# RWKV attention, then balanced experts: a fourth expert's first layer by seven products, a GpSimd drain behind the last gather, the last block's results in two halves

## The chip, the cores and the metric
The kernel runs on one core of a Trainium2 chip. Its time is device microseconds for one execution, the median of several runs. TensorE does the matrix products, VectorE (DVE) and ScalarE (ACT) work on tiles, GpSimd (POOL) issues the indirect DMAs, SyncE (SP) issues the plain ones.

## The reference
Two parts follow each other. An RWKV-5 attention over 4 sequences of 768 steps gives 3072 rows of 384 numbers. A mixture of 8 experts then gives each row to one expert, exactly 384 rows each, and sends it through that expert's two layers:

```python
for idx in order:                      # all (token, expert) pairs by falling logit
    tok, e = int(idx) // E, int(idx) % E
    if assigned[tok] >= 0 or counts[e] >= cap:
        continue
    assigned[tok] = e
    counts[e] += 1
...
for e in range(E):
    mask = assigned == e
    h = np.maximum(x[mask] @ w1[e], 0.0)      # 384 x 384 by 384 x 1024
    out[mask] = h @ w2[e]                     # 384 x 1024 by 1024 x 384
```

All numbers are 32-bit floats.

## The kernel before
**Stages.** The first 115 us or so are the attention. Then come the experts, one after the other, in `Experts.run`. Which expert is full next, and with which rows, is found by a search on VectorE with small products on TensorE (`likely_steps`, lines 1026 to 1099): three rounds that count candidates, each with two products (L949, L960) between VectorE operations, then `acc` (L1072), which settles the expert's rows and is kept as `walk.taking`. Then `tokens` lists the row numbers, and `fetch` (L1535) gathers the rows by three indirect DMAs from GpSimd (`gather`, L1530) and loads the weights from SyncE (L1523).

**Numbers.** An expert with all its three blocks of 128 rows is called whole. The whole ones have n = 1 to 7; the fourth is n = 4. Two blocks of one expert are done during the attention ("early"), and its last block comes at the end as n = 8.

**What runs during what.** While `run` works on n, the search for n + 1 or for the one behind it is made. `later` is a generator whose steps are pulled by `next` at set points of n's work. For n = 3, nine steps are pulled; with the last of them the search that settles expert 5's candidate rows is over. At the start of n = 4 `ahead = next(...)` pulls the whole next search and `fetch(5)`.

**First layer.** Plainly (`hidden`, L1648) it is 8 x 3 products of 128 x 128 weights by 384 columns. By seven (`hidden_by_seven`, L1600) two of the three slabs of rows are multiplied as 2 x 2 blocks in seven products, the third slab is added in plain products: 11 block products, each in four parts of 192 columns. It needs four sums of weight blocks (`weight_sums`, L1572, 128 x 512 each), five sums of row blocks (`row_sums`, L1583, 128 x 192 each), six additions of results on VectorE (L1624) and copies and activations on ScalarE (L1616, L1620). Each 32-bit product shows as two MATMUL instructions in the trace. `FIRST_BY_SEVEN` (L1799) lists the experts that are done so: 2, 3, 6, 7. The weight sums of the next expert are put behind `summed`, an early sum of the second layer now under way; its row sums behind `walk.taking`.

**Second layer.** Two of the three blocks go by seven products (`seven`, L1711, with the S sums of hidden blocks and T sums of weight blocks, L1704), the third block plainly in `result` (L1787, sixteen instructions of 384 columns). For n = 6 and 7 all three blocks go by fifteen products (L1763).

**The next rows turned.** The rows of n + 1 are turned by DMA, except for n + 1 = 1 and 5 (`BY_TENSOR`), which TensorE turns (L1545) into PSUM and ScalarE copies. During n = 4 that turning stands in the second layer ahead of product P4 in the program.

**Order.** A planner at build time puts the instructions of each engine in order by expected times; at run time each engine keeps that order. `tc.issue_after(ins)` puts the instructions of its block behind `ins` in their engine's order, without a wait.

**The end.** After n = 8's `result` with `to is None` the results stand in `o_last`; a branch (L2023) decides whether the general path has to run, and then `x.scatter(o_last, tok_last, ...)` (L2040) writes the last 128 rows. The closing DRAINs and barrier carry line 2064.

Of the kernel before, what the change touches and what calls it, by code (L numbers as in the profile page):

```python
# [10 lines left out]
F32 = mybir.dt.float32  # L11
# [1452 lines left out]
def rwkv5_eagle_then_base_layer_balanced(  # L1464
# [12 lines left out]
    nc = tc.nc  # L1477
    N, DX = out.shape
    E, _, F = moe_w1.shape
# [4 lines left out]
    KF = F // 128  # L1484
# [7 lines left out]
    walk = Assignment(ctx, tc, LG, CAP, C)  # L1492
    out_rows = dram_disjoint_views(out, NT)
    o_last = keep.tile([128, DX], F32, name="o_last")
    tok_last = keep.tile([128, 1], I32, name="tok_last")
# [3 lines left out]
    class Experts:  # L1499
# [26 lines left out]
        def gather(self, n, tok, within=N):  # L1526
            nb = tok.shape[1]
            xg = self.turns[n % 2].tile([128, NC, DX], F32, name="xg")
            for c in range(nb):
                nc.gpsimd.indirect_dma_start(  # L1530
                    out=xg[:, c, :], out_offset=None, in_=x_dram[0:within, :],
                    in_offset=bass.IndirectOffsetOnAxis(ap=tok[:, c:c + 1], axis=0))
            return xg
# [251 lines left out]
                                         in_=o_sb, in_offset=None)  # L1785

        def result(self, c, hid, w2, tok, to):  # L1787
            o_ps = self.ps_o.tile([128, DX], F32, name="o_ps")
            for j in range(KF):
                nc.tensor.matmul(o_ps, hid[:, j, ts(c, 128)], w2[:, j, :], start=(j == 0), stop=(j == KF - 1))  # L1790
            if to is None:
                nc.scalar.copy(o_last, o_ps)
                nc.vector.tensor_copy(tok_last, tok[:, c:c + 1])
                return
            o_sb = self.o.tile([128, DX], F32, name="o_sb")
            nc.scalar.copy(o_sb, o_ps)
            self.scatter(o_sb, tok[:, c:c + 1], to)

        FIRST_BY_SEVEN = 2, 3, 6, 7  # L1799
        BY_TENSOR = 1, 5  # L1800

        def run(self, ahead, later, rows, pulls={}, xT=None):
            xT, lead = xT or self.turn(ahead), True
            row_sums = weight_sums = None
            while ahead:
                n, _, tok, w1, w2 = ahead
                nb = tok.shape[1]
                whole = nb == NC
                many = whole and n in (E - 2, E - 1)
                ahead = next((a for a in later if a), None)  # L1810
                if weight_sums and not row_sums:
                    with tc.issue_after(walk.taking.ins):
                        row_sums = self.row_sums(xT)
                sums = dict(row_sums, **weight_sums) if weight_sums else None
                row_sums = weight_sums = None
                after = ahead and ahead[0] in self.FIRST_BY_SEVEN and ahead[2].shape[1] == NC
                late, lead = lead and not many, False
# [31 lines left out]
                def progress(t):  # L1849
                    nonlocal weight_sums  # L1850
                    if after and t > 1.1 and not weight_sums:
                        with tc.issue_after(summed.ins):
                            weight_sums = self.weight_sums(ahead[3])
                    while due and t > due[0]:
                        due.pop(0)
                        next(later, None)
                        if many and not due:
                            turn()
# [4 lines left out]
                if sums:  # L1863
                    hid = self.hidden_by_seven(sums, sums, progress)
                    half(hid)
                else:
                    hid = self.hidden(w1, xT, nb * 128, half if whole else lambda hid: None, progress, late)
# [48 lines left out]
    with ExitStack() as whole:  # L1916
        x = Experts()
# [5 lines left out]
        with ExitStack() as part:  # L1923
# [20 lines left out]
            with tc.manual_schedule():  # L1944
# [13 lines left out]
                for m in (1, 5, 2, 5, 2, 6, 5):  # L1958
# [4 lines left out]
                tok = walk.tokens(first["place"])  # L1963
                walk.between = lambda: None
                xg = x.gather(1, tok)
                to = walk.in_order(tok)
# [7 lines left out]
                                                                tag=("kT_ps", "rT_ps")[c % 2]))  # L1974
# [10 lines left out]
        def later():  # L1985
            yield from search
            walk.bound(ident)
            now = second
            for n in range(2, 5):
                walk.book(now, first=True)  # L1990
                yield x.fetch(n, now["fmax"], walk.tokens(now["place"]))
                walk.leave(now)
                yield
                now = walk.new_outs()
                yield from walk.likely_steps(**now)
            was = now
            walk.book(was)
            walk.leave(was)
            for n in range(5, E):
                rest = n == E - 1  # L2000
                yield
                if rest:
                    yield
                    now = walk.remainder()
                else:
                    now = walk.new_outs()
                    yield from walk.likely_steps(**now)
                walk.book(now, surely=rest)
                walk.choose(was, now)
                yield x.fetch(n, was["fmax"], walk.tokens(was["place"]))  # L2010
                if not rest:
                    walk.leave(now)
                was = now
            yield
            yield
            tc.mark_branch_hint_location("whole")
            have["ok"] = walk.found()
            yield x.fetch(E, walk.star, walk.tokens(walk.star_place, 1))

        x.run(ahead, later(), (a for a in [*out_rows[2:NT - 1], None]),  # L2020
              {1: 5, 2: 7, 3: 9}, xT)

    with tc.If(have["ok"] < 1, label="whole", preferred_fallthrough_block=False):  # L2023
# [3 lines left out]
        with ExitStack() as arm:  # L2027
            x = Experts()
# [40 lines left out]
```

## Time and profile before

| | us |
|---|---|
| median of 3 runs | 388.47 (388.26 to 389.25) |
| the profiled execution | 387.69 |
| its span, first to last instruction | 386.0 |
| TensorE busy | 369.8 |
| VectorE busy | 273.2 |
| ScalarE busy | 190.6 |
| GpSimd busy | 142.7 |

The profiled execution took 387.69 us, of which 386.0 lie between its first and last instruction. All points of time below are us from the start of that span. An instruction's row gives start, duration, engine, line, operation, output and inputs; in brackets, how long the engine stood idle before it and what ended that. "PEq", "POOLq" and the like are instructions of an engine's sequencer (waits, branches, DRAINs), which do not count as busy.

### The profile page before, as it was taken

The numbers are of one execution on the slowest core, as the hardware profiler recorded it, in microseconds if no ns is written. First come the engines' busy times: TensorE is split into PE (matmuls) and PEld (weight loads), VectorE is DVE, ScalarE is ACT, GpSimd is POOL, SyncE is SP. The second block draws the span as 40 slices with busy tenths as digits, with TensorE's granted clock in tenths as the row PEclk, the third lists the DMA queues.
The fourth block names the chain that finished last, engine by engine and source line by source line (L and its number), as shares of the span: only waits on it lengthen the run. The fifth ranks groups of instructions, "written<-read, shape, count | busy, mean of one in ns | idle before, by whom it ended". The sixth has DMA issues, their size and how long they took to land.

```text
span 386.0 us, 9900 instructions
## 1 busy us (share of the span) xinstructions
PE 369.8 (96%) x3769; PEld 305.2 (79%) x3769; DVE 273.2 (71%) x942; ACT 190.6 (49%) x474; POOL 142.7 (37%) x174
## 2 busy tenths in 40 slices
PE   7799999999998999999999999999999999999992
PEld 6677888888887765678898899558757889989981
DVE  6756876576885577988779869868367965995530
ACT  4997989888883312226344453322222636434220
POOL 7878987767742004032122131203213421060031
PEclk9999999999999999999999999999999999999998
DMA  7989888787592156474374392209208574590110
GB/s 145 192 171 208 184 176 186 151 178 155 109 374 90 43 172 243 143 259 103 117 292 80 90 344 48 77 0 333 96 21 313 157 257 173 103 348 21 24 65 28
DMA packets 108137, 60.53 MB, mean 157 GB/s; under 512 B 90032, under 2 KB 102320, under 8 KB 108080
## 3 DMA queue, kind: packets, MB, share of 16 engines
q1 hardware_dynamic: 104736, 50.35, 47.6%
q0 software_dynamic: 3104, 9.44, 7.0%
q8 instruction: 32, 0.52, 0.6%
q14 instruction: 25, 0.20, 0.2%
q10 hardware_dynamic: 240, 0.00, 0.0%
HBM read 47.20 MB, written 9.44 MB: 147 GB/s over the span
## 4 chain that ended last, share of the span: by engine, by line
PE 58%; issue 16%; DVE 9%; POOL 6%; DMA 4%; ACT 4%; POOLq 1%; another core or an unknown queue 0%; SPq 0%; DVEq 0%
PE h_ps L1655 8%; PE o_ps L1790 5%; PE y_ps L547 5%; PE pa_ps L1729 5%; PE h_ps L1632 5%; PE hb_ps L1632 4%; PE g_ps L507 4%; DMA xg<-x_rows,tok 3%; PE pb_ps L1729 3%; PE e_h_ps L1899 3%; ACT AT L497 2%; PE x_ps L597 2%; PE kv_ps L526 2%; PE kT_ps L460 2%; PE lg_ps L577 2%
## 5 line engine op out<-in xcount | busy, mean ns | idle before, releaser
L497 ACT ACTIVATE AT<-ident,dd 128x128 f32<-128x128 f32 x192 | 59.7, 393 | 2.1 <-DVE dd L450 2.1
L1655 PE MATMUL h_ps<-xT,w 128*128 128x384 f32 (+1 forms) x216 | 56.7, 412 | 0.1
L1530 POOL DMA_INDIRECT xg<-x_rows,tok x22 | 22.6, 1026 | 86.6 <-DVE own_c L1456 33.3
L1784 POOL DMA_INDIRECT out_dram<-o_all,to x16 | 21.4, 1338 | 88.5 <-DVE o_all L1772 41.0
L1655 PEld LDWEIGHTS h_ps<-xT,w 128*128 128x128 f32 x216 | 33.4, 191 | 14.6 <-issue 1.9
L514 DVE COPY_PREDICATED AT<-mask,g_ps 64x512 f32<-64x512 uint8 (+1 forms) x48 | 32.5, 727 | 11.9 <-PE g_ps L507 10.4
L1658 ACT ACTIVATE hid<-h_ps 128x384 f32<-128x384 f32 (+1 forms) x32 | 13.9, 437 | 42.9 <-PE h_ps L1655 40.9
L1790 PE MATMUL o_ps<-w,hid 128*128 128x384 f32 x96 | 33.4, 491 | 0.0
L507 PE MATMUL g_ps<-rT,kT 48*64 48x128 f32 (+1 forms) x768 | 26.3, 255 | 1.8 <-DVE AT L514 1.0
L438 POOL TENSOR_TENSOR kss<-krs,wk 128x384 f32<-128x384 f32 x24 | 24.3, 1016 | 5.9 <-ACT krs L346 3.0
L547 PE MATMUL y_ps<-AT,vts 128*64 128x128 f32 x384 | 25.7, 276 | 0.0
L1790 PEld LDWEIGHTS o_ps<-w,hid 128*128 128x128 f32 x96 | 17.4, 190 | 9.9 <-issue 0.6
L445 POOL TENSOR_TENSOR rk<-rk,u_bc 128x384 f32<-128x384 f32 x24 | 24.1, 1005 | 1.9
L507 PEld LDWEIGHTS g_ps<-rT,kT 48*64 48x64 f32 x768 | 20.6, 132 | 5.1 <-PE unread_ps L420 0.9
L444 POOL TENSOR_TENSOR rk<-krs 128x384 f32<-128x384 f32 x24 | 24.5, 1020 | 0.0
L547 PEld LDWEIGHTS y_ps<-AT,vts 128*64 128x64 f32 x384 | 20.6, 137 | 1.0 <-issue 0.7
L1620 ACT ACTIVATE hid<-kept_P 128x384 f32<-128x384 f32 x24 | 12.6, 523 | 17.4 <-DVE kept_P L1624 16.9
L479 DVE TENSOR_TENSOR rT<-rT_ps,WR 112x512 f32<-112x512 f32 x23 | 15.7, 684 | 5.8 <-PE rT_ps L460 5.8
L450 DVE TENSOR_REDUCE dd<-rk 128x8 f32<-128x384 f32 x24 | 13.1, 546 | 7.3 <-POOL rk L445 7.2
L566 ACT COPY x<-y_ps 128x512 f32<-128x512 f32 x24 | 14.1, 586 | 7.6 <-PE y_ps L547 6.2
L460 PE MATMUL rT_ps<-ident,krs 128*112 128x128 f32 x96 | 14.9, 274 | 0.7 <-ACT krs L346 0.7
L1763 PE MATMUL p_ps<-W,H 128*128 128x128 f32 x128 | 15.3, 275 | 0.0
(339 smaller groups left out, 873.0 us busy)
## 6 DMA issues: line engine op xcount, KB each, us to landing
w<-in_moe_w_dram SPq DMA_DIRECT2D x18, 1536.0 KB
krs<-in_k_dram SPq DMA_DIRECT2D x24, 192.0 KB
krs<-in_r_dram SPq DMA_DIRECT2D x24, 192.0 KB
vts<-in_v_dram SPq DMA_DIRECT2D x24, 192.0 KB
x_rows<-xr SPq DMA_DIRECT2D x24, 192.0 KB
xg<-x_rows,tok POOLq DMA_INDIRECT x22, 4.8
xg<-xg SPq DMA_TRANSPOSE x16
out_dram<-o_all,to POOLq DMA_INDIRECT x16, 2.9
```

What stands on the lines that cost most here:

```text
L438: self.nc.gpsimd.tensor_mul(self.kss[:, n % self.NS].rearrange("p (g h) d -> p g h d", g=2)[:, :, :, 0:D], src, self.wk.rearrange("p (g h) ...
L444: nc.gpsimd.tensor_mul(rk, self.krs[:, n % self.NK, 1, 0:H, 0:D], self.krs[:, n % self.NK, 0, 0:H, 0:D])
L445: nc.gpsimd.tensor_mul(rk, rk, self.u_bc)
L460: self.nc.tensor.transpose(ps[0:PD + self.D, a, :], self.pair(t, a), self.ident)
L497: nc.scalar.mul(AT[:, z, a, :], self.ident, dd[:, h:h + 1])
L507: nc.tensor.matmul(g_ps[ts(i, PD), z, a, i * PD:], kT[rows, a, ts(i, PD)], rT[rows, a, i * PD:], start=True, stop=True)
L514: nc.vector.copy_predicated(out=AT[keys, :, :, steps], mask=mask, data=g_ps[keys, :, :, steps])
L547: nc.tensor.matmul(yv[q * PD:(q + 1) * PD, o // 2, o % 2, :], lhsT, rhs, start=(o // 2, q) not in seen, stop=stop, skip_group_check=True)
L1632: nc.tensor.matmul(ps[:, q, :], w[b][:, ts(p * Q + q, 128)], x[a], start=fresh, stop=(a, b) == pairs[-1], skip_group_check=True)
L1655: nc.tensor.matmul(h_ps[j][:, at], w1[:, f, ts(j, 128)], xT[:, f, at], start=(f == 0), stop=(f == KD - 1))
L1729: nc.tensor.matmul(ps, left[a][:, j, :], right[b][:, j, :], start=(j == 0 and name in ("P1", "P2", "P5")), stop=(j == KF // 2 - 1), skip_g ...
L1790: nc.tensor.matmul(o_ps, hid[:, j, ts(c, 128)], w2[:, j, :], start=(j == 0), stop=(j == KF - 1))
```

## The change
Expert 4 is put into `FIRST_BY_SEVEN`, so its first layer goes by seven products. For n = 4 alone (`SUMS_SOONER`) the row sums are put behind the `taking` that stood before the pull of the next search, not behind the one that this pull makes. `gather` keeps its last indirect DMA, and after the last `fetch` a GpSimd `drain` is put behind it. In `result`, the last block's 384 result columns are made in two halves, each with its own PSUM tile and copy, and `tok_last` is copied first.

```diff
-                nc.gpsimd.indirect_dma_start(
+                self.gathered = nc.gpsimd.indirect_dma_start(
...
         def result(self, c, hid, w2, tok, to):
+            if to is None:
+                nc.vector.tensor_copy(tok_last, tok[:, c:c + 1])
+                D = DX // 2
+                for k in range(2):
+                    o_ps = self.ps_o.tile([128, D], F32, name="half_ps", tag="o_ps")
+                    for j in range(KF):
+                        nc.tensor.matmul(o_ps, hid[:, j, ts(c, 128)], w2[:, j, ts(k, D)],
+                                         start=(j == 0), stop=(j == KF - 1))
+                    nc.scalar.copy(o_last[:, ts(k, D)], o_ps)
+                return
             o_ps = self.ps_o.tile([128, DX], F32, name="o_ps")
...
-            if to is None:
-                nc.scalar.copy(o_last, o_ps)
-                nc.vector.tensor_copy(tok_last, tok[:, c:c + 1])
-                return
...
-        FIRST_BY_SEVEN = 2, 3, 6, 7
+        FIRST_BY_SEVEN = 2, 3, 4, 6, 7
+        SUMS_SOONER = 4,
...
+                mark = walk.taking
                 ahead = next((a for a in later if a), None)
+                if n not in self.SUMS_SOONER:
+                    mark = walk.taking
                 if weight_sums and not row_sums:
-                    with tc.issue_after(walk.taking.ins):
+                    with tc.issue_after(mark.ins):
                         row_sums = self.row_sums(xT)
...
-            yield x.fetch(E, walk.star, walk.tokens(walk.star_place, 1))
+            star = x.fetch(E, walk.star, walk.tokens(walk.star_place, 1))
+            with tc.issue_after(x.gathered.ins):
+                nc.gpsimd.drain()
+            yield star
```

## Rows read from the trace of the kernel before

**Rows 1.** page, parts 1 and 4: engines' busy time; the chain that ended last
```profile
PE 369.8 (96%) x3769; PEld 305.2 (79%) x3769; DVE 273.2 (71%) x942; ACT 190.6 (49%) x474; POOL 142.7 (37%) x174
...
PE 58%; issue 16%; DVE 9%; POOL 6%; DMA 4%; ACT 4%; POOLq 1%; another core or an unknown queue 0%; SPq 0%; DVEq 0%
```

**Rows 2.** windows of three first layers: length, busy PE, PEld, DVE, ACT, POOL
```profile
184.72:200.24 15.52, 15.40 (x106) 14.81 (x104) 12.31 (x63) 6.97 (x14) 3.88 (x4) 1.00 0.70 253
...
246.13:263.06 16.93, 16.79 (x69) 9.44 (x68) 12.80 (x70) 3.91 (x8) 1.00 (x1) 1.00 0.12 33
...
279.28:295.97 16.69, 16.69 (x68) 9.52 (x66) 11.44 (x68) 3.91 (x8) 2.48 (x3) 1.00 0.35 116
```

**Rows 3.** chain of waits, pieces: start, us, what
```profile
233.70 1.30 PE pb_ps L1729 x8
...
274.22 5.16 PE o_ps L1790 x16
```

**Rows 4.** VectorE: groups (ns min/median/max), T sums, window, waits from 246 to 263
```profile
L1590 DVE TENSOR_TENSOR first_S<-xT x12: 349/350/355, 188.4 to 343.0; 128x192 f32<-128x192 f32 x12
...
L1579 DVE TENSOR_TENSOR first_T<-w x8: 685/687/693, 169.9 to 333.5; 128x512 f32<-128x512 f32 x8
...
L1624 DVE TENSOR_TENSOR kept_P<-kept_P,h_ps x8: 546/554/555, 192.5 to 352.3; 128x384 f32<-128x384 f32 x8
...
L1704 DVE TENSOR_TENSOR T<-w,T 128x768 f32<-128x768 f32 x4 | 3.8, 956 | 1.5 <-PE pa_ps L1729 1.5
...
231.00:246.00 15.00, 15.00 (x83) 12.32 (x83) 13.71 (x54) 6.73 (x12) 2.22 (x2) 1.00 0.29 67
...
DVE own L926 <- PE counts L949: 1.4, 2, 0.7
...
DVE most L1050 <- PE counts L960: 1.3, 2, 0.6
...
DVE full_e L1061 <- PE counts L960: 0.8, 1, 0.8
```

**Rows 5.** timeline: search settled, first gather, rows of n = 5 turned
```profile
258.53 0.24 DVE L1072 SCALAR_TENSOR_TENSOR acc<-em,fmax,past 128x24 bf16<-128x24 f32 x1
...
265.81 1.24 POOL L1530 DMA_INDIRECT xg<-x_rows,tok  x1 [17.73 <-DVE tok L1447]
...
271.46 1.13 PE L1545 MATMUL xT_ps<-ident,xg 128*128 128x128 f32 x6
...
272.76 0.49 PE L1545 MATMUL xT_ps<-ident,xg 128*128 128x128 f32 x3
```

**Rows 6.** chain of waits: the gather of n = 5's rows
```profile
265.81 5.60 DMA xg<-x_rows,tok
```

**Rows 7.** the end: L2064 by kind, timeline from 379, a copy of 192 columns
```profile
L2064 POOLq DRAIN  x3: 46/115/5287, 379.8 to 385.7; - x3
...
L2064 SPq EVENT_SEMAPHORE  x14: 17/28/7602, 375.1 to 385.9; - x14
...
L2064 SPq DRAIN  x3: 7/7/13, 383.8 to 385.4; - x3
...
379.13 0.48 ACT L1792 COPY o_last<-o_ps 128x384 f32<-128x384 f32 x1 [4.89 <-PE o_ps L1790]
...
380.05 0.97 POOL L1784 DMA_INDIRECT out_dram<-o_last,tok_last  x1 [7.91 <-ACTq L2023]
...
L1734 ACT COPY kept_P<-pa_ps x15: 318/318/321, 171.3 to 304.0; 128x192 f32<-128x192 f32 x15
```

**Rows 8.** GpSimd's last gather and wait, its first DRAIN, TensorE's branch
```profile
345.58 1.45 POOL L1530 DMA_INDIRECT xg<-x_rows,tok  x1 [0.30 <-issue]
...
367.92 0.98 POOL L1784 DMA_INDIRECT out_dram<-o_all,to  x1 [20.89 <-DVE o_all L1772]
...
L2055 POOLq DRAIN  x1: 183/183/183, 0.4 to 0.4; - x1
...
L2023 PEldq COMPARE_BRANCH  x2: 95/1792/3490, 375.0 to 379.3; - x2
```

## The prediction
> **What bounds the kernel now.** I read the page first, for who is busy: TensorE is busy 96% of the span, and the chain that ended last lies on it for 58% [rows 1]. So a microsecond taken from TensorE counts, unless something else then arrives late. Next I cut the span into the first layers of the experts: an expert whose first layer goes by seven products holds TensorE 15.52 us, the fourth (n = 4) and fifth (n = 5), done plainly, 16.93 and 16.69 us [rows 2]. Then the chain from 246 to 280, for what could be late: it does not run through n = 4's products at all. It waits for the gather of n = 5's rows, which starts at 265.81 and takes 5.60 us [rows 6], after which TensorE turns those rows at 271.46 [rows 5]. TensorE and the gather arrive together today, and the gather hangs on a search that VectorE makes during n = 4's first layer. Last I read the end, where no product is left: the last scatter starts at 380.05, but GpSimd's closing DRAIN, queued from 379.8, lasts 5.29 us, to 385.1 [rows 7].
>
> **Seven products for n = 4.** Removed: 8 x 3 products of 384 columns, each two instructions in the trace, 48 in all. Added: 11 block products x 4, two instructions each, 88 of 192 columns. Sixteen of 384 columns took 5.16 us, 0.32 each; eight of 192 took 1.30 us, 0.163 each [rows 3]. Half the columns cost half the time, so 48 x 0.325 = 15.6 us become 88 x 0.163 = 14.3 us: 1.3 us less.
>
> The Trainium skill has a rule against this: "TensorE: Matmul & The Clock Gate", Back-to-back issue gap, says that the spacing of matmuls in a stream is set by the weight load as well, and gives 81 ns at 128 columns and 131 ns at 512. By an estimate worked out along that line the narrow matmul would cost about 0.78 of the wide one, and 88 of them would be dearer than 48. The trace does not agree: 0.163 against 0.32 us.
>
> What the stage holds beyond its own products is 16.93 - 15.6 = 1.3 us in n = 4, where three rounds of the search go through TensorE, and 15.52 - 14.3 = 1.2 us in a seven-product stage, where about one round, the places and the list go through. The new stage has all of the search and seven-product form: between 14.3 + 1.2 = 15.5 and 14.3 + 1.2 + 1.3 = 16.8 us. I take 15.9, nearer to the first, because the search pieces are counted in both sums. Gain **1.0 us**, ends 1.4 and 0.1.
>
> VectorE pays for it: 4 weight sums of 0.69 us during n = 3's second layer, 5 row sums of 0.35 us at the start of n = 4, and 6 additions of 0.55 us inside it [rows 4], together 2.8 + 1.8 + 3.3 = 7.9 us. The added copies on ScalarE are hidden: it is busy 3.91 of 16.93 us in n = 4 and 6.97 of 15.52 in a seven-product stage [rows 2]. What covers VectorE: between 231 and 246 it is busy 13.71 of 15 us, but 3.8 us of that are T sums for n = 4's second layer (the group has eight in two rows of four; half of them stand before 246), wanted only after 263, and can slide; between 246 and 263 it stands still 1.4 + 1.3 + 0.8 = 3.5 us waiting for counts [rows 4]. So the 2.8 us can push T sums back and 3.5 us of the rest can fill waits: the search ends later by d = 7.9 - 2.8 - 3.5 = 1.6 us. If every addition fits a wait badly, or the slid T sums fall ahead of the search, d is up to 1.6 + 3.5 = 5.1; if T sums slide far and additions fall behind the search, 0. I take d = 2.5, because a wait of 0.6 to 0.8 us holds one addition of 0.55 but not always at the right moment.
>
> The chain that this meets: the search settles its expert at 258.53, the first of three gathers starts at 265.81, and the last block is turned from 272.76 to 273.25 [rows 5]. With d = 2.5 it is turned by 275.8 and copied 0.48 us later (the copy of 384 columns in [rows 7]), by 276.2. TensorE could begin n = 5, which starts at 279.28 today [rows 2], at 278.3. Meanwhile it has 5.16 us of o_ps products [rows 3] and one product of 1.30 us, none of which needs the gather. So d up to about 4 costs nothing, **provided that those are put ahead of the turning**, which stands before them now. The order is made anew when the program is built, and today's has turning and products interleaved, as if made for landings of that moment; I take it that it follows. The weights of n = 5 come from the same search; they have more room than the rows, whose last landing is followed by turning.
>
> SUMS_SOONER moves only the row sums of n = 4: with the old mark they would stand behind the settling at 258.53, 12 us into the layer that needs them (its window begins at 246.13); with the new one behind the search settled during n = 3. It costs nothing itself. What queues behind the row sums on VectorE is the start of the search, counted in d.
>
> **The drain.** It is issued behind the last gather, which starts at 345.58; GpSimd then has nothing to do until 367.92, one wait of 20.9 us [rows 8]. Even at the 5.29 us of the closing one it is covered, and the three scatters queued behind it wait for VectorE anyway. Its benefit is not in the trace and has to be bounded. The closing DRAIN ends 5.05 us after the last scatter starts. The first of SyncE's closing waits begins at 375.1 and the longest, for that scatter's rows, lasts 7.60 us, so it ends about 382.8 [rows 7]; the DRAIN runs on 2.3 us. A DRAIN with no indirect DMA before it lasted 0.18 us [rows 8]. Two readings: the 2.3 us are the upkeep of all indirect DMAs since the start (24 blocks gathered and scattered, 48), 48 ns each as an estimate, of which an early DRAIN would take 44 away and leave 0.2 us; or they are fixed, and stay. In the first case GpSimd no longer ends last but SyncE, whose DRAIN comes at 383.8. The gain is at most 385.1 - 383.9 = **1.2 us**, at least 0; a loss is excluded by the 20.9 us wait. I take 1.2: the 0.18 us row is nearer to a price that grows with what is outstanding.
>
> **Halves.** The last block's 16 products of 384 columns become 32 of 192, equal time by rows 3. What follows them is a copy of 192 columns at 0.32 us instead of 384 at 0.48 us [rows 7]: 0.16 us. The first copy lies beside the second half's products. Against it stands the longer instruction stream before a branch. TensorE's branch there, begun at 379.3, lasts 3.49 us [rows 8], so TensorE itself ends near 382.8, when SyncE's wait ends too; part of the 0.16 may be lost. I take **0.1 us**, ends 0.16 gained and 0.3 lost (twice the gain, for want of a row). The copy of tok_last on VectorE moves forward into idle time.
>
> **Sum.** 1.0 + 1.2 + 0.1 = 2.3 us. The profiled execution took 387.69 us (span 386.0 and 1.7 around it): 385.4. The median of the three runs is 0.78 above that execution, so I forecast 388.47 - 2.3 = 386.2 us.
>
> **Rivals.**
> *The drain buys nothing.* Then the 2.3 us are fixed work of a DRAIN behind a scatter. For it: nothing in the trace separates the two. Time 388.47 - 1.1 = 387.4. Chance 0.20. The Trainium skill has a mechanism that would give this result, in "Runtime: NRT & Kernel Launch", Instruction fetch mechanics: a taken branch outside the prefetched pages stalls for a page. TensorE's 3.49 us branch would agree; for GpSimd it speaks less, since its DRAIN was already under way when the time went by.
>
> *The products' gain is eaten, the drain works.* VectorE is the bound of n = 4: its 12.80 us [rows 2] and 1.8 + 3.3 us more make 17.9, and the additions free the banks that TensorE needs. If they run late TensorE stays at 16.9 us. Time 388.47 - 1.3 = 387.2. Chance 0.15. Against it: the stage of n = 2 carries 12.31 us of VectorE work in its 15.52 [rows 2], so additions between search steps are nothing new.
>
> *Slower: the turning of n = 5's rows stays ahead of the other products.* Then n = 5 starts at 279.28 + d and not sooner, whatever n = 4 saved. With d = 2.5 the sum is +2.5 - 1.3 = +1.2, time 389.7; with d = 5.1 it is 392.3. It turns into a loss from d = 1.3 on. For it: today's order has the turning first, with the products behind it. Against: the order is made from expected landings. Chance 0.10.
>
> *Nothing happens:* both gains fail, 388.4. Chance 0.05.
>
> **How the numbers follow.** The forecast has 0.50. Its own range, by the ends of its terms, is 385.7 (1.4 + 1.2 + 0.16 = 2.8) to 387.5 (0.1 + 1.2 - 0.3 = 1.0). The range that should hold the time 8 times in 10 takes in the first two rivals and some spread of the runs (388.26 to 389.25 before): 385.1 to 387.9. About 0.3%, 1.2 us, is what a measurement of this kernel tells from no change; faster means below 387.3. Faster: the forecast's 0.50, half of the eaten gain and a third of the idle drain, 0.65. Same: what is left of those two and nothing happening, 0.25. Slower: the late turning, 0.10.
>
> **What would show it.** Right: n = 4's first layer near 15.9 us with 88 narrow products; the gather of n = 5 two to three us later against the start of n = 4's second layer, and o_ps products between that layer's seven and the turning; n = 5 starting about 1 us sooner; the closing DRAIN ending near SyncE's; a DRAIN of several us behind the gather at 345. Wrong: TensorE waiting for xg before turning; VectorE additions held up and TensorE waiting on ScalarE or VectorE in n = 4; a closing DRAIN still 5 us behind the start of the last scatter.

## The result: 1% slower

The changed kernel takes 392.83 us (median of 6 runs, 391.86 to 394.29). The kernel before took 389.07 in the same comparison (388.26 to 389.72). The ratio is 1.0103, 95% interval 1.0073 to 1.0132. I had forecast 386.2 us and given "slower" a chance of 0.10.

The profiled execution took 394.29 us, with a span of 392.6. The two spans differ by 6.6 us, where the medians differ by 3.8. The profiled execution is the slowest of the six, with a mean granted clock of 0.984, while the two runs at 0.998 and 0.999 took 392.0 us, so that about 2.9 us of the loss is there at full clock. The starts and ends of TensorE's stages in both traces say where the 6.6 us lie:

| stretch | before, us | after, us | difference |
|---|---|---|---|
| attention, to the start of n = 1 | 152.09 | 153.38 | +1.29 |
| n = 1 to n = 3 | 94.04 | 93.75 | -0.29 |
| first layer of n = 4 | 16.93 | 16.21 | -0.72 |
| second layer of n = 4 | 16.22 | 22.86 | **+6.64** |
| first layer of n = 5 | 16.69 | 16.69 | 0 |
| second layer of n = 5 | 14.53 | 15.47 | **+0.94** |
| n = 6 to the end of the last product | 68.6 | 68.6 | 0 |
| from there to the end of the span | 6.9 | 5.6 | **-1.3** |

The page's busy times and its chain (parts 1 and 4), to be held against [rows 1]:

```profile
PE 373.2 (95%) x3825; PEld 315.4 (80%) x3825; DVE 279.4 (71%) x957; ACT 194.0 (49%) x481; POOL 141.7 (36%) x174
...
PE 60%; DVE 11%; issue 10%; DMA 7%; POOL 6%; ACT 4%; POOLq 1%; SPq 0%; another core or an unknown queue 0%; DVEq 0%
```

TensorE is busy 3.4 us more although the change gives it less work, and the shares of DMA and VectorE in the chain have grown. Windows of the changed kernel (length, busy PE, PEld, DVE, ACT, POOL with counts, granted clock, DMA share, GB/s), for a stretch of the attention, the two layers of n = 4 and a stretch inside the second:

```profile
14.40:17.80 3.40, 3.40 (x54) 3.07 (x47) 2.57 (x5) 2.95 (x12) 3.32 (x5) 0.51 1.07 214
247.13:263.34 16.21, 16.14 (x104) 14.71 (x103) 14.65 (x69) 6.99 (x14) 0.97 (x1) 1.00 0.04 14
263.34:286.20 22.86, 19.17 (x97) 14.99 (x95) 14.13 (x64) 3.52 (x9) 5.59 (x5) 0.85 0.51 182
277.30:284.10 6.80, 5.62 (x15) 3.87 (x16) 0.36 (x1) 1.44 (x3) 1.12 (x2) 0.50 0.20 63
```

The second layer of n = 4 in the kernel before (its first is in [rows 2]):

```profile
263.06:279.28 16.22, 16.09 (x94) 13.26 (x89) 8.88 (x26) 3.52 (x9) 5.36 (x5) 1.00 0.62 234
```

The first row of the changed kernel is the 1.29 us of the attention: 3.4 us at half the granted clock (the level of 1.2 GHz). It is no part of the change: the profiled execution of the kernel with nothing but the drain (below) has the same stretch at 0.50, and that of "results first" (below), whose attention is the one of the changed kernel, has it at 1.00. From here on, "shifted" takes such a difference at the start of n = 1 off a time. The second row is what was hoped for: n = 4's first layer is 0.72 us shorter. The third is the loss: TensorE is busy 19.17 us of 22.86 where it had 16.09 of 16.22, and 6.8 us of the stage run at half clock. The GpSimd and TensorE rows there, against [rows 5]:

```profile
271.92 0.97 POOL L1784 DMA_INDIRECT out_dram<-o_all,to  x1 [22.92 <-DVE at L1035]
273.19 0.99 POOL L1530 DMA_INDIRECT xg<-x_rows,tok  x1 [0.30 <-DVE eq L926]
...
272.32 0.81 PE L1800 MATMUL o_ps<-w,hid 128*128 128x384 f32 x2
...
274.43 0.81 PE L1800 MATMUL o_ps<-w,hid 128*128 128x384 f32 x2
278.48 0.90 PE L1545 MATMUL xT_ps<-ident,xg 128*128 128x128 f32 x3 [3.24 <-DMA xg<-x_rows,tok]
279.18 1.48 PE L1800 MATMUL o_ps<-w,hid 128*128 128x384 f32 x2
280.46 1.48 PE L1545 MATMUL xT_ps<-ident,xg 128*128 128x128 f32 x6
281.74 4.57 PE L1800 MATMUL o_ps<-w,hid 128*128 128x384 f32 x10
```

The gather starts at 273.19, behind a scatter, 7.4 us later than before (6.1 shifted). TensorE stands for 3.24 us in front of the turning while twelve o_ps instructions that need nothing from the gather stand behind it. When the rows come, they run at half clock until 284.1: the last ten take 4.57 us, where sixteen took 5.16 in [rows 3].

Why the gather is late stands in VectorE's rows (the T sums are those of [rows 4]):

```profile
234.04 0.68 DVE L1579 TENSOR_TENSOR first_T<-w 128x512 f32<-128x512 f32 x1
...
238.11 0.95 DVE L1704 TENSOR_TENSOR T<-w 128x768 f32<-128x768 f32 x1
...
242.43 0.95 DVE L1704 TENSOR_TENSOR T<-w,T 128x768 f32<-128x768 f32 x1
...
248.76 0.24 DVE L1072 SCALAR_TENSOR_TENSOR acc<-em,fmax,past 128x24 bf16<-128x24 f32 x1
...
263.89 0.24 DVE L1072 SCALAR_TENSOR_TENSOR acc<-em,fmax,past 128x24 bf16<-128x24 f32 x1
271.56 0.16 DVE L1447 TENSOR_REDUCE tok<-mine 128x3 int32<-128x12 f32 x1
```

The same two points in the kernel before, the search during n = 3 settled and the list done:

```profile
243.77 0.24 DVE L1072 SCALAR_TENSOR_TENSOR acc<-em,fmax,past 128x24 bf16<-128x24 f32 x1
...
265.38 0.16 DVE L1447 TENSOR_REDUCE tok<-mine 128x3 int32<-128x12 f32 x1
```

The four weight sums (first_T) and the four T sums all stand ahead of the search that is settled during n = 3, at 248.76. Before, that point came at 243.77: 3.7 us later, shifted. The next search, which holds the row sums and all six additions, adds only 0.4 (263.89 against 258.53, 4.1 shifted). The list of rows takes 0.8 us more (263.89 to 271.56, against 258.53 to 265.38). The scatter that now stands ahead of the gather costs 1.2. The sum is 6.1.

The end, against [rows 7] (durations min/median/max in ns, first and last start):

```profile
L2030 POOLq DRAIN  x1: 7360/7360/7360, 351.5 to 351.5; - x1
...
L2077 POOLq DRAIN  x3: 46/115/3207, 387.7 to 392.3; - x3
L2077 SPq DRAIN  x3: 7/7/13, 391.6 to 392.0; - x3
```

The closing DRAIN lasts 3.21 instead of 5.29 us, and SyncE's is now the later one, at 391.6. The added DRAIN (L2030) ends at 358.9, in the wait that was meant to cover it.

### The profile page after: what moved, and what is told of

The parts are those of the page before. It is cut to its first block, busy times and chain, and to the rows that moved or that the text cites. A ratio compares the mean times of both kernels' runs of the same rounds, so it can differ in the third digit from the quotient of the medians.

```text
span 392.6 us, 10044 instructions
## 1 busy us (share of the span) xinstructions
PE 373.2 (95%) x3825; PEld 315.4 (80%) x3825; DVE 279.4 (71%) x957; ACT 194.0 (49%) x481; POOL 141.7 (36%) x174
## 4 chain that ended last, share of the span: by engine, by line
PE 60%; DVE 11%; issue 10%; DMA 7%; POOL 6%; ACT 4%; POOLq 1%; SPq 0%; another core or an unknown queue 0%; DVEq 0%
PE o_ps L1800 7%; PE h_ps L1655 7%; PE h_ps L1632 6%; PE y_ps L547 6%; PE hb_ps L1632 5%; PE pa_ps L1729 4%; PE g_ps L507 4%; DMA w<-in_moe_w_dram 3%; DMA xg<-x_rows,tok 3%; PE e_h_ps L1909 3%; ACT AT L497 2%; PE kv_ps L526 2%; PE pb_ps L1729 2%; PE x_ps L597 2%; PE hc_ps L1632 2%
## 5 line engine op out<-in xcount | busy, mean ns | idle before, releaser
L1784 POOL DMA_INDIRECT out_dram<-o_all,to x16 | 19.9, 1246 | 108.6 <-DVE o_all L1772 41.0
L1655 PE MATMUL h_ps<-xT,w 128*128 128x128 f32 (+1 forms) x168 | 40.0, 388 | 0.1
L1655 PEld LDWEIGHTS h_ps<-xT,w 128*128 128x128 f32 x168 | 24.8, 191 | 9.4 <-issue 1.2
L1800 PE MATMUL o_ps<-w,hid 128*128 128x384 f32 x80 | 30.6, 518 | 0.9 <-DVE o_all L1719 0.9
L547 PE MATMUL y_ps<-AT,vts 128*64 128x128 f32 x384 | 26.6, 282 | 0.0
L1620 ACT ACTIVATE hid<-kept_P 128x384 f32<-128x384 f32 x30 | 15.7, 523 | 20.7 <-DVE kept_P L1624 20.2
L1658 ACT ACTIVATE hid<-h_ps 128x384 f32<-128x384 f32 (+1 forms) x24 | 10.1, 420 | 30.0 <-PE h_ps L1655 29.5
L1800 PEld LDWEIGHTS o_ps<-w,hid 128*128 128x128 f32 x80 | 15.2, 203 | 8.7 <-issue 1.9
L1632 PE MATMUL h_ps<-xT,w 128*128 128x192 f32 x80 | 17.1, 335 | 0.0
L1632 PE MATMUL h_ps<-first_S,first_T 128*128 128x192 f32 x80 | 17.0, 333 | 0.1
```

Of the source, the lines that this page charges most:

```text
L547: nc.tensor.matmul(yv[q * PD:(q + 1) * PD, o // 2, o % 2, :], lhsT, rhs, start=(o // 2, q) not in seen, stop=stop, skip_group_check=True)
L1632: nc.tensor.matmul(ps[:, q, :], w[b][:, ts(p * Q + q, 128)], x[a], start=fresh, stop=(a, b) == pairs[-1], skip_group_check=True)
L1655: nc.tensor.matmul(h_ps[j][:, at], w1[:, f, ts(j, 128)], xT[:, f, at], start=(f == 0), stop=(f == KD - 1))
```

## The experiments

Ratios are to the kernel before on the same chip, with 95% intervals. The chips of these runs gave medians of 387.1 to 387.3 us for the kernel before, 1.8 us less than in the comparison above, so ratios are to be compared and not times. A part of that shows in the traces: from n = 6 to the last product every one of these kernels took 68.2 us, not 68.6.

### The parts alone

**Drain and halves**, and **the drain only**, **the halves only**, **the seven products only**. The first is the changed kernel with

```diff
-        FIRST_BY_SEVEN = 2, 3, 4, 6, 7
+        FIRST_BY_SEVEN = 2, 3, 6, 7
```

and the next two leave out the other half of its tail as well; the last keeps `FIRST_BY_SEVEN` and `SUMS_SOONER` and has the old tail.

> Fourth expert's first layer plain again; the drain and the two halves stay. My theory: all of the loss comes from the fourth expert, and the tail alone is better. The span from the last product's start to the end was 6.9 us before and 5.6 us after, so this kernel is 1.2 to 1.3 us faster than before (ratio 0.9967), with the closing DRAIN near 3.2 us and n = 5 starting as before. Rival: a part of the loss comes with the drain (it shifts the order of the scatters or the start of the program); then the time is within 0.5 us of before or above it.

> Only the drain behind the last gather is added. My theory: a DRAIN costs about 2 us and 0.047 us for each indirect DMA since the last DRAIN (5.05 us behind the last scatter's start with 48 of them before, 3.0 us with 4 of them after). So: early DRAIN ends some 4 us behind the last gather's end, the closing one 3.0 us behind the last scatter's start, time 1.2 us less than before. Rival: the closing DRAIN is shorter because the halves changed what precedes it; then the drain alone changes nothing and its closing DRAIN stays at 5.3 us.

> Only the last block's results in two halves. My theory: the copy falls from 0.48 to 0.32 us, but the last scatter starts 0.44 us behind the copy's end in before and 0.60 us in after, so nothing is left: between 0.2 us faster and 0.2 us slower, closing DRAIN at 5.3 us. Rival: the halves carry the tail's gain; then 1.2 us faster.

> Only the fourth expert's first layer by seven products (with its row sums sooner); no drain, no halves. My theory: n = 4's first layer takes 0.7 us less, n = 5 starts 5.5 to 7 us later than before since its gather starts 6 to 7.5 us later, n = 5's second layer costs 0.9 us more: 4 to 5.5 us slower than before, 1.2 us slower than the whole change. Rival: the drain or the halves have a share in the late gather; then 3 us slower or less.

| kernel | median, us | ratio |
|---|---|---|
| drain and halves | 386.83 | 0.9994 (0.9983 to 1.0004) |
| drain only | 386.24 | 0.9973 (0.9962 to 0.9983) |
| halves only | 387.25 | 1.0001 (0.9991 to 1.0011) |
| seven products only | 394.32 | 1.0176 (1.0157 to 1.0195) |

The loss comes from the seven products alone, and it is larger than I expected: 7.1 us, against 4 to 5.5. Its gather starts at 271.92 shifted, as in the whole change (271.90), and n = 5's second layer costs 1.25 us more than before; 1.05 us of the profiled execution are the attention's half clock, which I had not counted. In three of its four runs the mean granted clock was 0.985 to 0.987, and these took 394.3 to 394.4 us; in the fourth it was 0.997, and that run took 392.89, 5.6 us more than before. Why the loss is larger on this chip than in the first comparison stays open. The drain brings 1.0 us, the halves nothing.

The miss is the first kernel: drain and halves together should have brought at least what the drain brings, and brought 0.2 us by the ratio, 0.4 by the medians. The closing rows of the drain with the halves, then of the drain alone, and of the halves alone (same columns as above):

```profile
L2077 POOLq DRAIN  x3: 46/115/3286, 379.3 to 384.0; - x3
L2077 SPq DRAIN  x3: 7/7/13, 383.4 to 383.7; - x3
L2077 ACTq DRAIN  x2: 80/108/136, 382.2 to 384.6; - x2
```

```profile
L2071 POOLq DRAIN  x3: 46/115/3272, 380.5 to 385.2; - x3
L2071 SPq DRAIN  x3: 7/7/13, 384.6 to 384.9; - x3
L2071 ACTq DRAIN  x2: 8/44/81, 383.4 to 384.9; - x2
...
L2071 SPq EVENT_SEMAPHORE  x14: 17/28/8005, 375.4 to 385.4; - x14
...
L2071 ACTq EVENT_SEMAPHORE  x2: 17/17/17, 384.8 to 386.3; - x2
```

```profile
L2074 POOLq DRAIN  x3: 46/115/5286, 379.3 to 385.2; - x3
```

With the drain the closing DRAIN is 2.0 us shorter, with or without halves; with the halves alone it is not. But in the first kernel ScalarE's second closing DRAIN comes at 384.6, 0.9 us behind SyncE's at 383.7, and the end waits for it. With the drain alone both come at 384.9, but there ScalarE's very last instruction, an EVENT_SEMAPHORE, comes at 386.3, 0.9 us behind SyncE's at 385.4, so this execution ends as late. It is the slowest of its eight runs (387.78 us), and whether the others have the lateness too was not profiled. That ScalarE is what takes the drain's gain away in the first kernel is therefore likely, but not shown.

### Is ScalarE late because of the halves?

```diff
                     nc.scalar.copy(o_last[:, ts(k, D)], o_ps)
+                    if k == 0:
+                        for i in range(8):
+                            nc.scalar.copy(self.o.tile([128, 8], F32, name="spare"), o_last[:, 0:8])
```

> The kernel of drain and halves, with eight small copies (8 columns, result unread) on ScalarE between the two copies of the halves, while it waits for the second half. In the kernel of drain and halves ScalarE's second closing DRAIN came 0.9 us behind those of the other engines (384.65 against 383.75) and the end waited for it. My theory: this is the arrival of ScalarE's instructions behind its branch, and hangs on the place of that DRAIN in its stream; eight instructions more move it, ScalarE comes with the others again or is late at another instruction, and if it comes with the others the time is 0.9 us below that kernel's (about 0.997 of before). Rival: it hangs on the halves themselves; then the DRAIN is late by 0.9 us again and the time stays at 0.9994.

386.63 us, ratio 0.9976 (0.9962 to 0.9990).

```profile
L2080 SPq DRAIN  x3: 7/7/13, 384.4 to 384.7; - x3
...
L2080 ACTq DRAIN  x2: 8/44/80, 383.3 to 384.7; - x2
```

Eight more instructions on ScalarE and it comes with the others. By the ratios 0.7 us of the 0.9 are back, by the medians 0.15, and the intervals of the two kernels overlap, so the time does not settle it. The rows do settle that the halves alone are not what delays ScalarE: it comes with the others in five more kernels that have the drain and the halves (in the changed kernel at 392.0, as SyncE does, and in the four of the section on the late gather), and the drain alone, without halves, was late by 0.9 us one instruction further on. (With the halves alone it is 0.3 us late, 385.2 against 384.9.) That it hangs on where ScalarE's stream of instructions stands behind the branch fits all of these, but is argued and not shown. The Trainium skill, "Runtime: NRT & Kernel Launch", Instruction fetch mechanics, has a mechanism for this: instructions come in pages, and a taken branch out of the pages at hand waits for one. That a longer stream changes the delay agrees with it; the trace has three packets of instruction queues between 382.3 and 384.7 in the kernel of drain and halves, but does not say for which engine, so no run here shows the fetch itself.

### What does a DRAIN wait for?

To the kernel of drain and halves one more DRAIN is added, behind the last gather of n = 5:

```diff
             xg = self.gather(n, tok)
+            if n == 5:
+                with tc.issue_after(self.gathered.ins):
+                    nc.gpsimd.drain()
```

> The kernel of drain and halves, with one more DRAIN behind the last gather of n = 5, when 17 gathers and some 12 scatters are behind it. My theory: a DRAIN ends 1.9 us and 0.047 us for each indirect DMA since the last DRAIN behind the GpSimd row ahead of it: the new one 3.2 to 3.3 us behind the gather of n = 5, the one behind the last gather, with some 15 left, about 2.6 us behind it instead of 4.0, the closing one unchanged near 3.0 us behind the last scatter's start. Rival: the early DRAIN waits for the rows of the gather ahead of it to land; then both end some 4 us behind their gather.

Its two early DRAINs, then the last gather of n = 5 and the last gather of all, then the gathers' times from issue to landing (last column, median us; first those of n = 5, then the last one):

```profile
L1539 POOLq DRAIN  x1: 8128/8128/8128, 265.6 to 265.6; - x1
L2033 POOLq DRAIN  x1: 6163/6163/6163, 343.6 to 343.6; - x1
```

```profile
268.64 0.95 POOL L1530 DMA_INDIRECT xg<-x_rows,tok  x1 [0.30 <-issue]
...
345.53 1.44 POOL L1530 DMA_INDIRECT xg<-x_rows,tok  x1 [0.30 <-ACT kept_P L1619]
```

```profile
xg<-x_rows,tok POOLq DMA_INDIRECT x3, 4.6
...
xg<-x_rows,tok POOLq DMA_INDIRECT x1, 3.5
```

Both expectations are half right. The DRAIN behind the last gather, with 16 indirect DMAs since the one before it, ends at 349.8, 2.8 us behind the end of that gather's row; with 44, in the changed kernel, it ended 4.0 us behind it. That is 43 ns for each of 28, against 47 ns from the closing DRAIN (5.05 less 3.0 us behind the last scatter's start, for 44). So the number counts. But the DRAIN of n = 5, with 28, ends at 273.7, 4.1 us behind its gather where I expected 3.2 to 3.3. The rows of that gather landed near 273.2 (268.64 + 4.6, the median of the three), 0.5 us earlier. A floor set by the landing fits this one; a second point that would separate landing and number was not run. The time of its one run is 386.37 us, against 387.21.

### The late gather or the order behind it?

**Results first**: the rows of n = 5 are turned behind all of n = 4's o_ps products.

```diff
...
+                if n == 4:
+                    with tc.issue_after(self.made.ins):
+                        turn()
```

(`made` is the last of these products; the turning ahead of P4 is left out.) **Sums later**: the four weight sums of n = 4 stand behind the search.

```diff
-                    if after and t > 1.1 and not weight_sums:
+                    if after and t > 1.1 and not weight_sums and n != 3:
...
+                        if n == 3 and not due:
+                            with tc.issue_after(walk.taking.ins):
+                                weight_sums = self.weight_sums(ahead[3])
```

**All three**: both, and the scatters of an expert's first two blocks behind the gather.

```diff
...
-                self.leave(o_sb[:, c, :], tok[:, c:c + 1], next(rows))
+                with tc.issue_after(self.gathered.ins):
+                    self.leave(o_sb[:, c, :], tok[:, c:c + 1], next(rows))
```

**Kept busy**: the whole change with six idle products between n = 4's seven and the turning.

```diff
...
+                    with tc.issue_after(self.made.ins):
+                        for j in range(6):
+                            made = nc.tensor.matmul(h_ps, hid[:, j, ts(2, 128)], w2[:, j, :], start=(j == 0), stop=(j == 5))
+                    with tc.issue_after(made.ins):
+                        turn()
...
```

> The whole change, but n = 5's rows are turned only after all 14 o_ps instructions of n = 4's third block. My theory: the loss is made by the order on TensorE, 12 of these behind turnings that wait for the gather, and by the half clock that follows the wait. The gather stays as late as in after (start 273.2 in its clock, search settled 263.9); before, the last turning ended 7.4 us behind the first gather's start and its copy 0.5 later, so n = 5 starts near 281.1 instead of 286.2: 5 us less than after, about 0.9966 of before, and no half clock near 277. Rival: the late gather alone carries the loss; then n = 5 starts within 1.5 us of 286 and the time stays near 1.010 of before.

> The whole change, but the four weight sums of n = 4 stand behind the search that is settled during n = 3 (2.4 us of VectorE moved past it). My theory: those sums, and four T sums that did not slide, made the gather late. The search settles about 3.5 us sooner than in after, the first gather starts 4.5 to 6 us sooner (one scatter of 1.2 us falls behind it again), n = 5 starts between 279.5 and 281.5 in after's clock: 5 us less than after, about 0.997 of before. Rival: VectorE as a whole is too full, and what is moved behind the search pushes the next one; then the gather still starts at 271 or later, and n = 5 gains less than 2 us.

> Weight sums behind the search, the turning behind the results, and the scatter of n = 4's first blocks behind the gather. My theory: nothing of the late gather is left on TensorE's path; n = 4 keeps 0.7 us of its shorter first layer, n = 5 starts 0.3 to 1 us sooner than before, and the tail keeps up to 1.2 us: 0.995 to 0.9975 of before. Rival: the search is still 1 to 2 us later than before, n = 5 starts no sooner, and only the tail's gain stays: 0.997 to 1.000.

> The whole change, and six more products of 384 columns (12 instructions, result unread) on TensorE between n = 4's seven and the turning of n = 5's rows, where it stood for 3.2 us and more. My theory: the clock halves because TensorE stood still, so here it stays at full level, and what follows the first landing (9 turnings, 14 o_ps instructions, 6.1 us at full clock) ends at about 284.6 in after's clock, 1.6 us sooner than 286.2 although one product more comes behind the wait. Rival: the clock falls for another reason; then it is at half for some 6.8 us again and n = 5 starts near 287.

| kernel | first gather, shifted | start of n = 5, shifted | median, us | ratio |
|---|---|---|---|---|
| before | 265.81 | 279.28 | | 1 |
| after | 271.90 | 284.91 | | |
| results first | 271.91 | 280.50 | 388.68 | 1.0036 (1.0025 to 1.0047) |
| sums later | 269.33 | 283.40 | 393.01 | 1.0154 (1.0124 to 1.0184) |
| all three | 269.34 | 279.43 | 388.04 | 1.0037 (1.0020 to 1.0054) |
| kept busy | 271.91 | 283.84 | 391.56 (one run) | |

Results first, TensorE:

```profile
273.18 4.68 PE L1800 MATMUL o_ps<-w,hid 128*128 128x384 f32 x14
277.69 0.82 PE L1545 MATMUL xT_ps<-ident,xg 128*128 128x128 f32 x6
...
279.44 0.52 PE L1545 MATMUL xT_ps<-ident,xg 128*128 128x128 f32 x3 [0.88 <-DMA xg<-x_rows,tok]
280.53 0.91 PE L1655 MATMUL h_ps<-xT,w 128*128 128x384 f32 x2 [0.57 <-ACT xT L1546]
```

The gather is as late as in the whole change, to 0.01 us, and n = 5 starts 4.4 us sooner. So most of the 6.64 us is the order, with what follows from it, the half clock among that. The time is a miss all the same, 1.0036 where I expected about 0.9966: n = 5 still starts 1.2 us late, and its second layer takes 15.87 us, 1.34 more than before. Sums later is a miss as well, 1.0154 for an expected 0.997. The search during n = 3 is back in its place, and the scatter is behind the gather again, which explains the 2.6 us that the gather gains; but the next search, with the weight sums now beside it on VectorE, loses 2.6 us where it had lost 0.4. The order on TensorE looks as if made for a still earlier landing:

```profile
271.96 0.49 PE L1729 MATMUL pa_ps<-T,hid 128*128 128x192 f32 x2
275.79 0.55 PE L1545 MATMUL xT_ps<-ident,xg 128*128 128x128 f32 x3 [3.34 <-DMA xg<-x_rows,tok]
...
278.74 0.52 PE L1545 MATMUL xT_ps<-ident,xg 128*128 128x128 f32 x3 [1.42 <-DMA xg<-x_rows,tok]
```

It now stands 3.34 and 1.42 us in front of two turnings, with fourteen of the sixteen o_ps instructions behind them. The rival's limit (less than 2 us gained at n = 5) holds, but not with its late gather, and for a reason that neither theory had.

Kept busy, granted clock in the stretch from the first turning to n = 5, against 0.50 in the row of after:

```profile
277.27:283.84 6.57, 6.01 (x25) 3.53 (x25) 0.00 (x0) 1.44 (x3) 0.17 (x1) 1.00 0.13 49
```

With TensorE at work in the wait, the clock stays in this one run. That standing still is what brought it down is not shown by that alone, since in the profiled execution of sums later it stayed at 1.00 behind the 3.34 us as well. The same stretch took 7.72 us in after (278.48 to 286.20) and 6.57 here, with one product of 0.65 us more in it: the half clock cost about 1.8 us.

All three together bring n = 5 back to 0.15 us of its old start, and yet the kernel is slower than before, outside my range (0.995 to 0.9975) and the rival's (0.997 to 1.000). Its n = 5 second layer takes 15.70 us, 1.17 more than before, which eats the tail's gain. (Its profiled execution, 387.51 us, is the fastest of its eleven and 0.4 us above the median of before; the median lies 0.5 us higher, and what the others lose beyond that was not profiled.) Its row of waits in n = 5's second layer, and three rows of VectorE there in the changed kernel, which has the same wait (0.9 us):

```profile
PE o_ps L1801 <- DVE o_all L1719: 1.1, 1, 1.1
```

```profile
309.53 1.29 DVE L1579 TENSOR_TENSOR first_T<-w 128x512 f32<-128x512 f32 x2 [0.88 <-DMA w<-in_moe_w_dram]
310.74 0.69 DVE L1579 TENSOR_TENSOR first_T<-w,first_T 128x512 f32<-128x512 f32 x1
311.34 0.35 DVE L1719 TENSOR_TENSOR o_all<-kept_P,pb_ps 128x192 f32<-128x192 f32 x1
```

The weight sums of n = 6 wait for their weights, and the addition that frees a bank of PSUM for TensorE stands behind three of them.

### Is that all of it?

**Five corrections**: all three, the halves left out, and n = 6's weight sums behind that addition.

```diff
...
-                    if after and t > 1.1 and not weight_sums:
-                        with tc.issue_after(summed.ins):
+                    if after and t > (1.7 if n == 5 else 1.1) and not weight_sums and n != 3:
+                        with tc.issue_after(self.third.ins if n == 5 else summed.ins):
```

**Two turned sooner**: in addition, two of the three blocks of n = 5 are turned ahead of the last two o_ps products (four instructions), which hides their copies.

```diff
...
+                    if j == 6 and self.hook:
+                        with tc.issue_after(self.made.ins):
+                            self.hook()
+                            self.hook()
+                        s.enter_context(tc.issue_after(self.turner.ins))
...
```

(`hook` turns one block, `turner` is its last turning.)

> All three changes of order; the halves taken out; and n = 6's weight sums put behind the addition of n = 5's third product, which stood behind two of them while they waited for the weights (TensorE waited 1.1 us for that addition, 1.2 us in n = 5's second layer). My theory: this is the last of the loss, so n = 6 starts where it did before, and with the drain the kernel is 0.8 to 1.3 us faster than before: 0.9965 to 0.998. Rival: n = 6 starts late for another reason (its weights land late); then it stays above 0.9995.

> The kernel of the five corrections, with the first two blocks of n = 5 turned ahead of the last four of n = 4's o_ps instructions, the third block behind them. There TensorE ended its o_ps products at 277.85, turned three blocks, stood 0.24 and 0.57 us for copies of turned rows, and began n = 5 at 280.08. My theory: with two turnings and their copies beside the last products, one turning of 0.5 and one copy of 0.5 us are left behind the products, n = 5 starts 0.5 to 0.8 us sooner, and the kernel comes to 0.996 to 0.9968 of before, the first in which the seven products of n = 4 bring something. Rival: the second block has not landed by then (its gather starts at 271.28 and takes 1.93 us on GpSimd, two late ones in a row), TensorE waits for it ahead of the last products, and nothing is won or 0.5 us lost.

Five corrections took 386.30 us, ratio 0.9978 (0.9967 to 0.9989); two turned sooner took 385.93 us, ratio 0.9967 (0.9955 to 0.9979). Both lie in the ranges expected of them. Windows of n = 4's two layers in each (columns as above), and n = 5's second layer in the first:

```profile
246.76:262.88 16.12, 15.97 (x103) 14.68 (x102) 14.43 (x62) 6.36 (x13) 1.80 (x1) 1.00 0.03 12
262.88:280.08 17.20, 16.39 (x95) 13.34 (x93) 14.08 (x55) 4.33 (x11) 8.00 (x6) 1.00 0.70 241
...
296.82:311.21 14.39, 14.39 (x75) 12.01 (x74) 10.81 (x19) 6.84 (x12) 2.88 (x3) 1.00 0.56 168
```

```profile
246.32:262.44 16.12, 15.97 (x104) 14.68 (x102) 14.43 (x62) 6.36 (x13) 1.80 (x1) 1.00 0.03 12
262.44:279.24 16.80, 16.29 (x94) 13.23 (x93) 13.34 (x52) 4.39 (x11) 7.27 (x6) 1.00 0.71 247
```

n = 5's second layer is back at 14.39 us. n = 4 as a whole takes 33.32 us in the first kernel, 32.92 in the second and 33.15 before. So even in a good order the seven products bring 0.23 us of the 0.81 that they save in the first layer; the rest is paid back in the second, where the gather is still 3.5 us late. And 0.23 us hardly stands out: in the five other profiled kernels whose n = 4 is plain, n = 4 took 33.02 to 33.35 us. The last kernel is faster than the kernel before and the changed one, but the drain alone is not told apart from it (0.9973, 0.9962 to 0.9983).

## Why the prediction was wrong, step by step

**Seven products.** Right: 0.72 us of a forecast 1.0 (ends 1.4 and 0.1). By the rule of the Trainium skill that I had weighed ("TensorE: Matmul & The Clock Gate", Back-to-back issue gap) the stage would have become longer; the trace does not agree, it became shorter.

**The lateness d, the term that failed first.** I took 2.5 us, ends 0 and 5.1; measured at the gather it was 6.1. The part inside n = 4 was right: row sums and additions filled waits, and the search lost 0.4 us there. What failed is the step "the 2.8 us can push T sums back". Not one T sum moved behind the search; all four weight sums were added in front of it, and 3.7 us came of 2.8. And d ended at the search: I had not priced the list behind it (0.8 us more, with four S sums of n = 4's second layer among its instructions where two had stood) nor asked what else would be ready on GpSimd by then (a scatter, 1.2 us).

**The condition "provided that those are put ahead of the turning".** It did not hold. Four of the sixteen o_ps instructions went ahead of the turning, twelve stayed behind. I had written that "I take it that it follows": the order did move with the later gather (none of the sixteen stood ahead before), but by far too little; which landing it was made for no run shows. This was my slower rival. Its mechanism was right: TensorE waits for the gather with free products behind the wait. That its sum with the measured d comes so close, 279.28 + 6.1 = 285.4 for a measured 284.9 shifted, is partly luck: the rival had neither the half clock (1.8 us more) nor the four o_ps instructions that did go ahead of the turning (4 x 0.32 = 1.3 us less), and both fell into the same stage. Its chance of 0.10 was wrong. A condition that I could not read from the trace of before, on which the sign hung, deserved near an even chance. An experiment shows this step: with the order alone corrected (results first), 4.4 us come back at the same late gather.

**What the sum lacked.** The half clock behind the wait, about 1.8 us in the profiled execution, though not in every run: the two at full clock still took 392.0 us, so the loss does not need it. And n = 5's second layer, 0.94 us, one stage past the place where I stopped looking, where a wait for weights on VectorE holds an addition that TensorE needs.

**The drain.** Right in size and reading: 1.2 forecast, 1.0 measured alone (0.27%). The closing DRAIN is 2.1 us shorter and SyncE ends last. The price of 48 ns for each indirect DMA came out at 43 to 47 in two of three comparisons; the third DRAIN ended later than that, as if it had a floor, which I had not seen.

**Halves.** 0.1 us forecast (ends 0.16 and -0.3), nothing measured alone. Beside the drain they cost 0.8 us by the ratios (0.9994 against 0.9973), 0.6 by the medians, which is outside my ends. ScalarE's late DRAIN is the likely cause, but the profiled execution of the drain alone has a lateness of the same size, so it stays open. I had named the longer stream before a branch as the risk, but on TensorE. In the changed kernel itself ScalarE is not late, and there the tail won 1.3 us.

## What to carry to other kernels

When work is added to an engine that makes the next stage's inputs late, price the whole chain down to the transfer, and check what stands behind the waiting instruction on the engine that receives it: the same late gather cost 5.6 us with twelve free instructions behind the wait (about 1.8 of them the half clock), and 1.2 with none. A saving in one stage is kept only if the next stage's input comes sooner by as much; here 0.8 us of saved products became some 0.2. A shorter end only counts up to the next engine that is late there, so look at all five engines' closing rows, down to each one's last instruction.

## What was not expected of the hardware

TensorE's granted clock fell to half at 277.3, about 2 us into a wait of 3.2 us, and stayed there until 284.1, 5.6 us into the work that followed; it did not fall when idle products filled the wait. It does not follow every such wait: in the profiled execution of sums later TensorE worked at full clock behind a wait of 3.34 us. In that of the seven products only, behind a wait of 3.38 us, it fell 0.2 us after the work had begun again and stood at 0.50 from 278.6 to 282.0. What decides this stays open.

A GpSimd DRAIN's time grew with the indirect DMAs since the last one, 43 ns each from 16 to 44 of them and 47 ns each from 4 to 48; one DRAIN, with 28, took longer than that and ended 0.5 us behind the landing of its gather. And ScalarE's closing DRAIN came 0.9 us behind the others' in one kernel and with them in the same kernel with eight small instructions more in front of it.
